# A retention block with a feed-forward behind it: a copy in another place, one k transposed by TensorE, natural k issued later

## The chip, the core and the metric

One core of a Trainium2 chip runs the whole program. The metric is the time of one execution on the device in microseconds (us); of several executions the median is given. Engines go by the names of the profile: PE is TensorE, DVE VectorE, ACT ScalarE, POOL GpSimd, SP SyncE (which here only issues transfers). ACT and POOL issue transfers too, and an engine's instructions run in the order of the program.

## What is computed

```python
# q, k, v: (8, 8, 576, 64) float32
scores = q @ k^T / 8
gamma  = 1 - 2 ** (-5 - arange(8))                    # one decay per head
D[s, t] = gamma ** (s - t) if s >= t else 0
x = ((scores * D) @ v), heads put side by side         # (4608, 512)
a, b = x @ w1, x @ w2                                  # (4608, 1024) each
out = ((a * b) @ w3) @ w_out                           # (4608, 512)
```

The weights and the inputs w1, w2, w3, w_out arrive as 64-bit floats and are turned into 32-bit ones on the chip; all products are in 32-bit.

## The kernel before

**Attention.** Batches are taken in pairs, and the 576 positions of a pair in five pieces (64, then 4 x 128). One piece of a pair is a *unit* `g`; there are 20, numbered from 0 (unit 10 is the eleventh, and the first, short piece of the third pair). Each unit needs k and q transposed (`kT`, `qT`), k as it lies in memory ("natural k", `ld_k`) for the running state, and v (`ld_v`). `state` (L240) adds k^T v to the state, `score` (L224) makes the masked scores `pm`, `pv` (L278) makes the unit's piece of x and copies it to `xT`. Transposed q and k come in two ways. Either SP loads the tensor in 32x32 blocks (`load_blocks`, L160: 8 or 16 transfers of 32 KB into a tile `bl_q` or `bl_k`; both kinds share two buffers with the tag `ld_q`) and DVE transposes the blocks (`front_blocks`, L185), or TensorE transposes natural k against an identity into PSUM and ACT copies it out (`front`, L207). `scale_blocks` (L175) lets POOL scale q.

**Feed-forward.** x is multiplied with w1 and w2 by Strassen's seven products: the first four of its twelve blocks of 384 tokens in `up` (L507), with one level; the other eight, in four groups of two, in `up2` (L1008), with two levels. w3 and w_out are multiplied once into `w3o`, and `down` (L625) multiplies a pair of token tiles with it, in seven products of four 128x256 matrix products each. Its first result is copied by ACT (L667), its sums are added by DVE (L641, L681), S4 is formed by DVE (L679), ACT copies one product out (L682) and issues the stores of the result tile `ot` (L710), of which there is one buffer.

**`up2`.** A group of tokens takes 14 multiplications of seven products; the seventh product is put off (`behind`) and issued by `finish()` inside the next `up2` or `down`. The sums of weights ("forms", 896 KB for a multiplication) are made once, sent to memory (`kept`, L882 to L888) and read back into a ring of three places (`next_forms`, L935: `ra<-kept`, L939). SP issues the first two of these loads in `open_second`, POOL all others, each in an `up2` for the multiplication after the next. The place ring[0] lies in the tile `ra` where the weights wA0 lay; ring[1], ring[2] and the two places `first` lie in the second tile `ra`, where the weights wA1 lay. The sums of tokens are made by POOL in `token_forms` (L942, operations at L948): `E` first, the forms `u` next; the last of the first group, `E4` (L969), comes in `rest()`, after a `down`. POOL also adds the second-level sums (L1033, `more`), DVE the others (L1038, L1040), and DVE multiplies a with b (L1003).

**Order.** Nothing is scheduled automatically. `work(n)` (L1099) takes the next `up`, `up2` or `down` from the list `todo`. Small steps are laid into lists which a multiplication empties as it goes: `aside`, `spread`, and `beside` (scaling of v by ACT). The stage change comes around unit 10: `down` on tiles (1,0),(1,1); loads for unit 10; `open_first` (L909), which sends the last weight forms; `token_forms(0)`; `down` on (2,2),(3,2); `open_second` (L921), which gives wA1's place to the ring and to `first`; `rest()`; and `down` on (3,0),(3,1), the first in which `second` is true. In it, and in every later `down`, L667 writes into `live["first"]` and not into `ot`; the stores and the product that the last `up2` left over come right behind it. Then `state(10)`, `score(10)` and the first `up2`, which begins with two 128x384 products that fill both `seed` buffers (L1016). Each later unit gets a number of multiplications (`dealt`, L1193); at its end come `pv(g)`, the loads of v and natural k for unit g + 2 by POOL (L1224, L1226), and state and score of unit g + 1. Units 11 to 13 (`whole`) get their transposed k from `front`.

Of the kernel before, what the change touches and what calls it, by code (L numbers as in the profile page):

```python
# [19 lines left out]
def kernel(  # L20
# [13 lines left out]
    nc = tc.nc  # L34
# [527 lines left out]

    aside, owed, spread, beside = [], [], [], []
    g = 0

    def w3_sums():
# [56 lines left out]
    def down(x, y, then=None, last=False):  # L625
        a, done, left = pair_of(x, y)
        second = "first" in live
        ahead(x, y)
        while len(done) < (1 if second else 3):
            aside.pop(0)()  # L630
        ps = {}
        ot = pools["ot"].tile([P, 2, 2, DM // 2], F32, tag="ot", name="ot")

        def product(nm, A, B, on=None):
            ps[nm] = ps[on] if on else acc.tile([P, DM // 2], F32, tag="acc", name="po")
            for f in range(NP):
                nc.tensor.matmul(ps[nm], a[A][:, f, :], live["W"][B][:, f, :], start=(f == 0 and not on),  # L637
                                 stop=(f == NP - 1), skip_group_check=True)

        def plus(nm, to, sb):  # L640
            nc.vector.tensor_add(ot[:, to[0], to[1]], ps[nm], ot[:, sb[0], sb[1]])  # L641
            if spread:
                spread.pop(0)()
            if second and aside and nm != 3:
                aside.pop(0)()

        def put(m, t, row, half=slice(0, 2)):

            i, n = every[m]
            r0 = t * P  # L650
            while r0 < (t + 1) * P:
                b = r0 // TB
                e = min((b + 1) * TB, (t + 1) * P)
                r = (2 * i + b) * S + n * TB + r0 - b * TB
                stores.append((out[r:r + e - r0, half.start * DM // 2:half.stop * DM // 2],
                               ot[r0 - t * P:e - t * P, row, half].rearrange("p h d -> p (h d)")))
                r0 = e
            if not keep_stores and not second:
                store()

        C11, C12, C21, C22 = (0, 0), (0, 1), (1, 0), (1, 1)
        product(1, "A11", "B11")
        first = ot[:, 0, 0]
        if second:
            first = live["first"].pop(0)
            live["first"].append(first)
        nc.scalar.copy(first, ps[1])  # L667
        if second:
            store()
            finish()  # L670
        product(7, "S3", "T3")
        if second:
            multiply()
        while len(done) < 3:
            aside.pop(0)()
        if then:
            ahead(*then)
        product(2, "A12", "B21", on=1)
        nc.vector.tensor_tensor(out=a["S4"], in0=a["A12"], in1=a["S2"], op=ALU.subtract)  # L679
        product(6, "S2", "T2")  # L680
        nc.vector.tensor_add(ot[:, 0, 1], ps[6], first)  # L681
        nc.scalar.copy(ot[:, 0, 0], ps[2])  # L682
        early = second or last or g >= 2 * NC - 1
        if early:
            put(*x, 0, slice(0, 1))
            store()
        plus(7, C21, C12)
        product(5, "S1", "T1")
        plus(5, C22, C21)
        product(4, "A22", "-T4")  # L690
        plus(4, C21, C21)
        put(*y, 1)
        if second:
            store()
        product(3, "S4", "B22", on=5)
        while aside and not early:
            aside.pop(0)()
        plus(3, C12, C12)
        put(*x, 0, slice(1 if early else 0, 2))
        if last:  # L700
            store()
        while aside:
            aside.pop(0)()
# [3 lines left out]
    def store():  # L707
        while stores:

            nc.scalar.dma_start(*stores.pop(0))  # L710
# [191 lines left out]
    ring, sent, steps, free = [], [0], [0], []  # L902
# [105 lines left out]
    def up2(gr, n):  # L1008

        h, key = n // 7, order[n % 7]  # L1010
        slot = ring[steps[0] % 3]
        if not steps[0]:

            for _ in range(2):
                t = pools["seed"].tile([P, 2, TB], F32, tag="seed", name="seed")
                nc.tensor.matmul(t.rearrange("p a t -> p (a t)"), ident, live["w3o"][:, 0, :2 * TB],  # L1016
                                 start=True, stop=True)
        B = live["B2", gr][OPERANDS[key][1]]
        steps[0] += 1
        c = free.pop(0)  # L1020
        sums2[key] = c
        add = {"P2": "P1", "P6": "P1", "P7": "P6", "P4": "P7", "P3": "P6"}.get(key)
        add = sums2[add] if add else None
        both = [sums2["P6"], sums2["P7"]] if key == "P5" else []

        def product(ps, a, b, new=False):
            for w in range(2):
                nc.tensor.matmul(ps[:, w, :], weight_of(slot, a, w), B[b], start=(new and w == 0), stop=True,  # L1028
                                 skip_group_check=True)

        def more(into, of, part):
            o, i = into[:, part], of[:, part]
            nc.gpsimd.tensor_tensor(out=o, in0=o, in1=i, op=ALU.add)  # L1033

        def plus(ps, j, with_add=None):
            if both:
                for o in both:
                    nc.vector.tensor_add(o[:, j], ps, o[:, j])  # L1038
            elif with_add is not None:
                nc.vector.tensor_add(c[:, j], ps, with_add[:, j])  # L1040
            else:
                nc.scalar.copy(c[:, j], ps)

        p1 = acc.tile([P, 2, TB], F32, tag="acc", name="up")
        product(p1, "A11", "B11", True)
        p6 = pools["seed"].tile([P, 2, TB], F32, tag="seed", name="seed")
        nc.scalar.copy(p6, p1)  # L1047
        store()
        p5 = acc.tile([P, 2, TB], F32, tag="acc", name="up")
        product(p5, "S1", "T1", True)  # L1050
        nc.scalar.copy(c[:, 3], p5)  # L1051
        finish()
        next_forms()
        product(p6, "S2", "T2")
        nc.scalar.copy(c[:, 1], p6)
        if beside:
            beside.pop(0)()
        for o in both:
            more(o, c, 3)
        if add is not None:  # L1060
            more(c, add, 3)
        product(p1, "A12", "B21")
        plus(p1, 0, add)
        product(p5, "S4", "B22")
        if add is not None:
            more(c, add, 1)
        for o in both:
            more(o, c, 1)
        product(p6, "S3", "T3")
        plus(p6, 3, c)  # L1070
        plus(p5, 1, c)
        if both:
            free.append(c)
        multiply(1 if both else 2)
        if n == 13:
            results.append((gr, h, 0, 1, c, 1))
        if aside:
            aside.pop(0)()

        def rest():  # L1080
            product(p6, "A22", "-T4")
            plus(p6, 2, add)
            if key in ("P6", "P3"):
                free.append(sums2["P1" if key == "P6" else "P6"])
            done = {"P2": (0, 0), "P4": (1, 0), "P5": (1, 1), "P3": (0, 1)}.get(key)
            if done:
                z = sums2["P7"] if key == "P5" else c
                results.extend((gr, h, *done, z, half) for half in ((0,) if n == 13 else (1, 0)))

        behind.append(rest)  # L1090
# [26 lines left out]
    g = NC  # L1117
# [48 lines left out]

    g = 2 * NC - 1
    work(1)
    for nm in "qk":
        load_blocks(g + 1, nm)  # L1170
    pv(g)()
    load(g + 2, "v", nc.scalar)
    load(g + 2, "k")
# [5 lines left out]
    g = 2 * NC  # L1179
    work(1)  # L1180
    rest()
    aside.extend(lambda nm=nm: front_blocks(g, nm) for nm in "qk")
    work(1)
    while aside:
        aside.pop(0)()
    ready = {2 * NC + 3: 1, 3 * NC + 1: 2, G - 1: 3}

    whole = range(2 * NC + 1, 2 * NC + 4)
# [5 lines left out]
    for g in range(2 * NC, G):  # L1194
        n = dealt[g - 2 * NC]
        if g + 1 < G:
# [6 lines left out]
            for nm in "qk":  # L1203
                blocks_in = nm == "q" or g + 1 not in whole
                if blocks_in:
                    aside.append(lambda nm=nm: front_blocks(g + 1, nm))
                work(1)
                while aside:
                    aside.pop(0)()
                if not blocks_in:  # L1210
                    front(g + 1, "k")
                if g + 2 < G and not (nm == "k" and g + 2 in whole):
                    load_blocks(g + 2, nm)
            work(tail)
            while beside:
                beside.pop(0)()
        else:
            work(n)
        pv(g)()
# [3 lines left out]
        if g + 2 < G:  # L1223
            load(g + 2, "v", nc.gpsimd)  # L1224
            if (g + 2) % NC != NC - 1:
                load(g + 2, "k", nc.gpsimd)  # L1226
        if g + 1 < G:
            state(g + 1)
            score(g + 1)
# [4 lines left out]
    g = G  # L1234
# [44 lines left out]
```

## Time and profile before

| | us |
|---|---|
| median of 5 runs | 861.39 |
| lowest and highest of them | 860.36, 876.87 |
| the profiled execution | 860.36 |
| its span, first to last instruction | 858.6 |
| granted TensorE clock, mean over the span | 0.991 |

| engine | busy us | share of the span |
|---|---|---|
| PE | 822.3 | 96% |
| DVE | 541.7 | 63% |
| POOL | 326.5 | 38% |
| ACT | 281.8 | 33% |

A profile line gives the start in us from the span's beginning, the length in us, the engine, the line of the program, the operation, the tile written and those read, the shape and the number of instructions, and in brackets the idle time of the engine before it with what ended that. An engine with a q behind its name (SPq, ACTq) stands for its issue of transfers. The waits view has who waited for whom, then us in total, how often, and the longest. Transfers have a time from issue to landing: the median is 5.0 us for the 54 loads `ra<-kept` that POOL issues.

### The profile page before, as it was taken

How to read it: one execution, taken by the hardware profiler on the slowest of the kernel's cores; microseconds unless marked ns; L12 is line 12 of the kernel's file. 1: busy time of each engine (PE TensorE's matmuls, PEld its weight loads, DVE VectorE, ACT ScalarE, POOL GpSimd, SP SyncE). 2: the span in 40 equal slices, each digit the busy share in tenths (PEclk: the TensorE clock that was granted, in tenths of full speed). 3: DMA queues.
4: the chain of work that ended last, by engine and by line, in shares of the span. 5: the costliest groups of instructions: out<-in, count | busy, mean ns of one | idle time of the engine just before them, and what ended most of it. 6: DMA issues, size and time to landing. Idle time of an engine off the chain costs nothing.

```text
span 858.6 us, 15769 instructions
## 1 busy us (share of the span) xinstructions
PE 822.3 (96%) x6077; PEld 739.3 (86%) x6077; DVE 541.7 (63%) x888; ACT 281.8 (33%) x579; POOL 326.5 (38%) x330
## 2 busy tenths in 40 slices
PE   9999999999999999499899999989999999999998
PEld 8899999644889998389898888988889998899987
DVE  4999999990744487335557643748744759446663
ACT  4777566771121111024244014242024331033300
POOL 1100010002004081567446754647925368535600
PEclk9999999999999999889999999999999999999999
DMA  9994454526055577979685437887355452245401
GB/s 190 224 225 115 76 152 119 148 74 110 13 111 104 101 250 232 280 191 219 169 232 162 68 81 201 224 214 196 66 110 196 152 206 68 83 147 178 166 25 50
DMA packets 203467, 127.22 MB, mean 148 GB/s; under 512 B 163448, under 2 KB 185208, under 8 KB 203392
## 3 DMA queue, kind: packets, MB, share of 16 engines
q1 hardware_dynamic: 173120, 50.40, 29.5%
q0 software_dynamic: 11776, 63.71, 22.9%
q10 hardware_dynamic: 18496, 12.10, 5.2%
q8 instruction: 48, 0.79, 0.4%
q14 instruction: 27, 0.22, 0.1%
HBM read 103.88 MB, written 22.28 MB: 147 GB/s over the span
## 4 chain that ended last, share of the span: by engine, by line
PE 75%; DMA 8%; DVE 8%; issue 4%; SPq 3%; ACT 1%; POOL 1%; DVEq 0%; ACTq 0%; POOLq 0%
PE po L637 22%; PE up L1028 15%; PE up L524 11%; PE seed L1028 11%; PE ps L477 6%; DMA ra<-kept 3%; PE xps L299 3%; DMA ld_v<-in_v_dram 3%; PE sc L233 3%; PE xps L274 1%; DVE c L529 1%; DVE ab L1003 1%; SPq L171 1%; SPq L882 1%; DMA kept<-wS 1%
## 5 line engine op out<-in xcount | busy, mean ns | idle before, releaser
L637 PE MATMUL po<-w3o,ab 128*128 128x256 f32 x552 | 127.0, 385 | 12.7 <-ACT ra L667 11.2
L637 PEld LDWEIGHTS po<-w3o,ab 128*128 128x128 f32 x552 | 105.0, 192 | 29.4 <-ACT ra L667 11.6
L1033 POOL TENSOR_TENSOR cc<-cc 128x384 f32<-128x384 f32 x112 | 109.5, 1004 | 4.0 <-ACT cc L1051 2.4
L1040 DVE TENSOR_TENSOR cc<-seed,cc 128x384 f32<-128x384 f32 x88 | 48.7, 553 | 73.6 <-PE seed L1028 71.5
L181 POOL TENSOR_TENSOR bl_q<-bl_q,gqs 128x512 f32<-128x512 f32 (+1 forms) x30 | 31.5, 1070 | 131.8 <-DMA bl_q<-in_q_dram 98.1
L939 POOL DMA_DIRECT2D ra<-kept x54 | 30.8, 570 | 128.4 <-PE seed L1028 102.5
L1028 PE MATMUL up<-xT,ra 128*128 128x192 f32 x384 | 73.5, 328 | 0.0
L524 PE MATMUL up<-xT,wA 128*128 128x192 f32 x384 | 70.7, 328 | 0.2 <-DVE xT L496 0.2
L1040 DVE TENSOR_TENSOR cc<-up,cc 128x384 f32<-128x384 f32 x88 | 48.4, 550 | 34.2 <-PE up L1028 28.6
L529 DVE TENSOR_TENSOR c<-up,c 128x384 f32<-128x384 f32 x80 | 44.0, 550 | 37.6 <-PE up L524 37.0
L637 PE MATMUL po<-wB,forms 128*128 128x256 f32 x288 | 65.4, 380 | 0.5 <-DVE forms L611 0.5
L236 DVE TENSOR_TENSOR pm<-sc,mask 128x512 f32<-128x512 f32 (+1 forms) x80 | 45.4, 626 | 31.8 <-PE sc L233 31.7
L524 PEld LDWEIGHTS up<-xT,wA 128*128 128x128 f32 x384 | 63.3, 190 | 1.6 <-issue 0.5
L1028 PEld LDWEIGHTS up<-xT,ra 128*128 128x128 f32 x384 | 63.8, 190 | 1.0
L637 PEld LDWEIGHTS po<-wB,forms 128*128 128x128 f32 x288 | 54.9, 191 | 8.4 <-PE po L637 0.8
L1028 PE MATMUL up<-ra 128*128 128x192 f32 x288 | 55.9, 331 | 6.3 <-DMA ra<-kept 6.2
L1047 ACT COPY seed<-up 128x384 f32<-128x384 f32 x56 | 26.0, 464 | 104.2 <-PE up L1028 48.7
L679 DVE TENSOR_TENSOR ab<-ab,forms 128x512 f32<-128x512 f32 x17 | 17.3, 1018 | 66.3 <-PE po L637 66.3
L477 PE MATMUL ps<-wo,w3T 128*128 128x512 f32 x128 | 55.1, 592 | 0.0
L1028 PE MATMUL seed<-e,ra 128*128 128x192 f32 x256 | 51.6, 330 | 3.5 <-DVE cc L1040 2.9
L1028 PEld LDWEIGHTS up<-ra 128*128 128x128 f32 x288 | 48.4, 192 | 7.5 <-DMA ra<-kept 6.0
L204 POOL TENSOR_TENSOR ld_v<-ld_v,gk 128x1024 f32<-128x1024 f32 (+1 forms) x9 | 17.4, 1930 | 91.6 <-DMA ld_v<-in_v_dram 91.6
(127 smaller groups left out, 1594.3 us busy)
## 6 DMA issues: line engine op xcount, KB each, us to landing
ra<-kept POOLq DMA_DIRECT2D x54, 896.0 KB, 5.0
raw<-in_moe_w_dram SPq DMA_DIRECT2D x72, 128.0 KB, 3.0
bl_q<-in_q_dram SPq DMA_DIRECT2D x216, 32.0 KB, 2.9
out_dram<-ot ACTq DMA_DIRECT2D x54, 128.0 KB, 2.3
bl_k<-in_k_dram SPq DMA_DIRECT2D x144, 32.0 KB, 3.0
raw<-in_moe_w_dram SPq DMA_DIRECT2D x16, 256.0 KB, 6.3
ld_k<-in_k_dram SPq DMA_DIRECT2D x8, 512.0 KB, 5.5
raw<-in_moe_w_out_dram SPq DMA_DIRECT2D x32, 128.0 KB, 2.7
```

What stands on the lines that cost most here:

```text
L181: nc.gpsimd.tensor_tensor(out=part, in0=part, in1=gqs[:, :, n0:n0 + n].unsqueeze(3).to_broadcast([P, NP, n, BL]), op=ALU.mult)
L233: nc.tensor.matmul(sc[j][:sz, p, :sz], kT[hs, b, p, :sz], qT[hs, b, p, :sz], start=True, stop=True)
L236: nc.vector.tensor_mul(pm[:sz, b, j, :, :sz], sc[j][:sz, :, :sz], mask[:sz, :sz].unsqueeze(1).to_broadcast([sz, NP, sz]))
L477: nc.tensor.matmul(ps, live["w3T", ft][:, g, :], live["wo"][:, g, :], start=(g == 0), stop=(g == KF - 1))
L524: nc.tensor.matmul(ps[:, w, :], a[:, w, r, :], b[:, r, :], start=(new and w == r == 0), stop=(w == r == 1), skip_group_check=True)
L529: nc.vector.tensor_add(c[:, to], ps, c[:, sb])
L637: nc.tensor.matmul(ps[nm], a[A][:, f, :], live["W"][B][:, f, :], start=(f == 0 and not on), stop=(f == NP - 1), skip_group_check=True)
L939: engine.dma_start(ring[n % 3], kept[n % 14 // 7][nm])
L1028: nc.tensor.matmul(ps[:, w, :], weight_of(slot, a, w), B[b], start=(new and w == 0), stop=True, skip_group_check=True)
L1033: nc.gpsimd.tensor_tensor(out=o, in0=o, in1=i, op=ALU.add)
L1040: nc.vector.tensor_add(c[:, j], ps, with_add[:, j])
L1047: nc.scalar.copy(p6, p1)
```

## The change

Three things are altered.

1. In the one `down` that comes before the first `up2` (`steps[0]` is 0), L667 writes into `ot[:, 0, 0]`, as it does in the downs of the first stage, and not into `live["first"]`. All later downs are as before.
2. Unit 10's k is not loaded in blocks. Its natural k, which was loaded for the state anyway, is transposed by TensorE: `front(10, "k")` stands behind that `down`. DVE's transpose of it goes, SP has 8 transfers fewer, and q of unit 11 takes the buffer that the blocks of k had.
3. The load of natural k for unit g + 2 is put into a list `loads`. The next `up2` issues it directly behind its own `next_forms()`, so on POOL it stands behind the load of weight forms and before the additions of L1033. If no `up2` comes in that unit, it is issued at the end of the unit's work, behind `scale_blocks` and `token_forms` (so for natural k of units 15 and 18). A unit whose k is transposed by `front` empties the list first.

```diff
-    aside, owed, spread, beside = [], [], [], []
+    aside, owed, spread, beside, loads = [], [], [], [], []
...
         first = ot[:, 0, 0]
-        if second:
+        if second and steps[0]:
             first = live["first"].pop(0)
...
         finish()
         next_forms()
+        if loads:
+            loads.pop(0)()
         product(p6, "S2", "T2")
...
     work(1)
-    for nm in "qk":
-        load_blocks(g + 1, nm)
+    load_blocks(g + 1, "q")
     pv(g)()
...
-    aside.extend(lambda nm=nm: front_blocks(g, nm) for nm in "qk")
+    aside.append(lambda: front_blocks(g, "q"))
     work(1)
     while aside:
         aside.pop(0)()
+    front(g, "k")
...
                 if not blocks_in:
+                    while loads:
+                        loads.pop(0)()
                     front(g + 1, "k")
...
-            while beside:
-                beside.pop(0)()
+            for left in (loads, beside):
+                while left:
+                    left.pop(0)()
...
-                load(g + 2, "k", nc.gpsimd)
+                loads.append(lambda g=g: load(g + 2, "k", nc.gpsimd))
```

## The prediction

> **What bounds the kernel now.** I read the page's busy times first, then who waited for whom, then the timeline where TensorE waits longest.
>
> ```profile
> PE 822.3 (96%) x6077; PEld 739.3 (86%) x6077; DVE 541.7 (63%) x888; ACT 281.8 (33%) x579; POOL 326.5 (38%) x330
> ```
>
> TensorE (PE) is busy for 96% of the span, so only its own work or its idle time can change the end. The waits view lists where it idles:
>
> ```profile
> PE po L637 <- ACT ra L667: 11.2, 1, 11.2
> ...
> PE up L1028 <- DMA ra<-kept: 6.2, 3, 2.8
> ```
>
> One wait of 11.2 us hangs on an ACT copy, three of 6.2 us together on the weight forms. The timeline of 318 to 400 us shows the first:
>
> ```profile
> 350.18 3.97 SPq L171 DMA_DIRECT2D bl_k<-in_k_dram  x8
> ...
> 350.50 3.72 PE L637 MATMUL po<-w3o,ab 128*128 128x256 f32 x16 [0.52 <-DVE ot L641]
> ...
> 363.50 1.77 SPq L939 DMA_DIRECT2D ra<-kept  x2
> 364.95 0.37 ACT L667 COPY ra<-po 128x256 f32<-128x256 f32 x1 [18.16 <-DMA kept<-wS]
> ...
> 365.38 3.78 PE L637 MATMUL po<-w3o,ab 128*128 128x256 f32 x8 [11.16 <-ACT ra L667]
> ...
> 366.95 1.80 POOL L948 TENSOR_TENSOR e<-xT,e 128x768 f32<-128x768 f32 x1
> ...
> 375.29 1.82 POOL L948 TENSOR_TENSOR e<-xT,e 128x768 f32<-128x768 f32 x1
> ...
> 377.05 0.62 POOL L939 DMA_DIRECT2D ra<-kept  x1
> ```
>
> TensorE ends two products at 354.22 and stands until 365.38. The copy writes into `ra`, which lies where the weights wA1 lay, and has to wait until the last of them has been sent to memory. The timeline of 392 to 416 us shows the largest of the three others:
>
> ```profile
> 395.26 1.20 POOL L93 DMA_DIRECT2D ld_v<-in_v_dram  x1 [2.00 <-PE xps L299]
> ...
> 396.46 1.17 POOL L93 DMA_DIRECT2D ld_k<-in_k_dram  x1
> ...
> 400.46 0.56 POOL L939 DMA_DIRECT2D ra<-kept  x1 [2.83 <-PE seed L1028]
> ...
> 410.25 1.65 PE L1028 MATMUL up<-ra 128*128 128x192 f32 x4 [2.79 <-DMA ra<-kept]
> 411.69 1.48 PE L1028 MATMUL up<-u,ra 128*128 128x192 f32 x4
> ```
>
> The form issued at 400.46 landed 9.7 us later, against a median of 5.0; v and k were ahead of it in GpSimd's queue. Behind the gap groups of four take 1.5 to 1.65 us instead of 0.81. Busy time by stretches prices gap and slow clock together, for two attention units with the same four multiplications (columns: length, PE, PEld, DVE, ACT, POOL, clock, DMA share, GB/s):
>
> ```profile
> 397.90:422.10 24.20, 21.41 (x124) 20.65 (x122) 12.84 (x23) 9.06 (x22) 13.76 (x16) 0.93 0.89 201
> 427.90:447.50 19.60, 19.57 (x122) 19.00 (x120) 11.52 (x21) 9.97 (x24) 10.44 (x13) 1.00 0.81 218
> ```
>
> That is 4.6 us, of which 2.79 are the gap and 1.8 the clock.
>
> **Part 1: the copy in its own place.** It now waits for product 1 (352.4) and for the stores of the pair of tiles before, which read the single `ot` buffer. Their last was issued at 350.5 and took 2.7 us: 353.2. With 0.37 us of copy it is done at 353.6, before TensorE asks at 354.22. The cover is only 0.6 us; each us of later stores would cost one. Five products of 8 matmuls at 0.216 us, 8.65 us, then follow at full clock (they took 10.75 behind the gap), and the pair ends at 362.9 instead of 376.1.
>
> **Part 2: k of unit 10 by TensorE.** Added are 8 transposes (the same 8 at 128 columns took 1.04 us; here 64, I take 0.9) and two ACT copies of about 0.33 us (as the 128x256 copies of L306), under the state products. One DVE transpose (0.70 us) goes, beside other work. SyncE loses 8 issues (3.97 us), so ld_k, the sends and the first two ring loads go out 4 us earlier: about 359.5 and 361, landed, at the 5.0 and 7.0 us of before, at 364.5 and 368. The load of q for unit 11 no longer waits for the buffer (372.65 before) and starts near 361; it may slow the second ring load by 1 us, which is not needed before 372. State, score and seeds took 3.4 us (376.1 to 379.5), so the first `up2` could start at 367.2, 12.3 us early.
>
> **What is late next** is GpSimd. Its chain of token forms starts when bl_q has landed (352.46), which neither part moves. E[0], for the second product, is ready at 368.75: up to 1 us of wait. E4, for the last product of the first `up2`, is ready at 377.1, and the load into the third ring place is queued behind it (377.05). The first `up2` then ends its six products near 372.4, the second does two (1.3 us) and stands from 373.7 to 377.2. Five products follow (3.25 us, plus 1.8 us of slow clock if the gap is treated as the one above): 382.2. The third `up2` needs the third ring place: 377.05 plus 5.0 (the median) to 6.7 us (this load before, with q loads beside it). I take 5.7, as the q of unit 11 is then in: 382.8. It started at 387.99 before. **Gain 5.2 us, from 3.6 to 6.0**, not the 12 that the gap suggests.
>
> Two rules of the Trainium skill bear on this. SBUF — State Buffer (Who interferes with whom) says that a DVE operation with two SBUF inputs holds up a GpSimd one that reads SBUF. The rows show that GpSimd can be slowed: the 128x384 sums take 0.98 us here, 1.44 in the later chains, under more DVE work. If any DVE work counted, the 3.6 us that now come under the chain (four masks, 1.41, and four additions of 0.55) would delay E4 by 1.6 us: the second chain took 25.2 us with 12.95 of DVE, this one 21.6 with 4.82, 0.44 us for each. By the rule, only L679 counts, which lay under the chain before as well (it took 1.47 instead of 0.69); the products' additions read PSUM. I take the rule, 0, and keep 1.6 for the range. TensorE: Matmul & The Clock Gate (Part 1) puts the fall to half clock at an idle window of about 3.4 us, running freely; by that the 2.79 us gap might have been free, but the row charges 1.8. I take the row for the new 3.5 us gap; by either sum the third ring place comes last, so it hides the loss.
>
> **Part 3: natural k behind the next form.** In four units (11, 12, 15, 16) the form now goes ahead of 512 KB; k's other two loads go behind a block of GpSimd work under the output products and are used later (that of unit 15 lands near 511 on the old clock, wanted at 515). GpSimd's form waits for TensorE anyway at 400.46 and 558.89, so there it isn't issued earlier, only freed of k's transfer; at 517.91 it followed k directly and comes 1.2 us earlier. Queued behind k's 1.17 us of issue are the additions of L1033, two q scalings and the next form: in unit 11 that one goes out near 406.2 instead of 405.0 on the old clock.
>
> - Unit 11: the form must land within 7.0 us; without k, and with the q loads earlier, I expect 5 to 6. The 4.6 us go. DMA: Bandwidth & Descriptors (Queues, rings and completion order) speaks against this: a ring is consumed in its order, so k, now behind this form, delays the next one. In the trace that form (405.01) took 9.2 us. By rule and bytes alone (v, k and two forms all in 16.3 us into the unit, at 414.2; the last wanted after three multiplications of 4.55 us and the transposes of k, 14.5) 1.8 us come back; by the share of q loads then gone, none. I take 4.5 (2.2 to 4.6).
> - Unit 12: 6.8 us before, no gap over 0.2: 0.
> - Unit 15: the form landed after 9.9 us, TensorE waited 1.17. Issued 1.2 us earlier, with only v ahead, it should take the 8.1 us of the form at 640.37, which had v alone ahead: gain 1.2 (0.6 to 1.3).
> - Unit 16: the form (9.1 us, gap 2.28) had v, k and 16 loads of bl_k beside it. The next took 8.5 us and landed 15.6 us into the unit; without the gap it is wanted at 13.65. So most comes back: 0.5 (0 to 2.4).
>
> **Sum.** 5.2 + 4.5 + 1.2 + 0.5 = 11.4 us. The profiled execution took 860.36 us (span 858.6 and 1.76 around it), so 849.0; the median of the five runs is 861.39, 1.0 above it, so I forecast 850.0 as a median.
>
> **The rivals.**
> - *The waits only move* (chance 0.20): k delays the second form in units 11, 15 and 16, and GpSimd's chain comes 1.6 us late. Gain 3.6 + 2.2 + 0.6 + 0 = 6.4: 855.0. For it: 9.2 and 8.5 us for those forms. Against: q loads are earlier by then.
> - *Most of the gap is kept* (0.04): the chain or third ring place doesn't bind; the third `up2` starts near 377, gain 11 + 6.2: 844. Against: GpSimd's order has E4 ahead of that load.
> - *Slower* (0.05): k in the ring makes the second form 2.8 us late in all four units, and the clock falls each time: (2.8 + 1.8) x 4 = 18.4, against 5.2 and the 8.1 us of old gaps removed: 866.5. It decides from 3.3 us per unit on. Against: unit 12 has no gap, though the same four transfers share its queue.
> - *No effect* (0.03): the stores or the ring hold TensorE until 365; 861. Against: they land at 353.2 and near 364.5, with other work between.
>
> **How the numbers follow.** The main case has 0.68; its terms span 6.4 to 14.3 us, and the range takes some of the first rival: 846.0 to 856.0. A difference under 0.2% (1.7 us) can't be told from none here. Faster 0.92, same 0.03, slower 0.05.
>
> **What would show it.** Right: no wait on L667; the new longest wait near there is TensorE on GpSimd (E4) for some 3.5 us, then under 1 us on the ring; the third `up2` 5 us earlier; unit 11 at 19.6 to 20 us. Wrong: L667 waiting on the stores, E4 after 379, or the second form of units 11 and 16 with waits over 2 us.

## The result, and the profile after

The changed kernel took 854.59 us (median of 23 executions, 849.51 to 859.90); the kernel before, beside it, 870.72 (44 executions, 858.85 to 877.30). The ratio is 0.9912, with an interval of 0.9887 to 0.9937. Executions of the kernel before lie at 858.9 to 865.0 and at 870.0 to 877.3, and the ratios here compare with the lower ones, but for a few executions up to 871.5. So the change is worth some 7.6 us of 861; 11.4 had been forecast.

The executions of the changed kernel fall into two groups: twelve from 849.5 to 854.6, eleven from 856.9 to 859.9. The profiled execution (857.14 us, span 855.4) is of the upper one. Its page, and its waits of TensorE over the whole span:

```profile
PE 822.0 (96%) x6085; PEld 738.8 (86%) x6085; DVE 546.7 (64%) x887; ACT 282.7 (33%) x581; POOL 326.1 (38%) x330
```

```profile
PE seed L1028 <- DVE cc L1040: 8.4, 4, 5.6
PE po L637 <- DVE ot L641: 3.4, 2, 2.9
...
PE po L637 <- ACT ot L667: 1.4, 2, 1.1
...
PE up L1028 <- DMA ra<-kept: 0.4, 1, 0.4
```

The wait of 11.2 us on L667 has shrunk to 1.1, and the three waits for weight forms (6.2 us) to one of 0.4. In their place stand one of 2.9 us on a sum of VectorE and one of 5.6 us on a sum for which GpSimd was late; the forecast had neither. Busy time by stretches shows unit 11, with the columns of the prediction:

```profile
403.46:423.25 19.79, 19.65 (x125) 18.98 (x122) 12.91 (x23) 9.06 (x22) 14.87 (x17) 1.00 0.86 220
```

Unit 11 now takes 19.79 us where it took 24.20, at full clock: gap and slow clock are both gone. So part 3 did what was expected, and the loss lies ahead of it. The timeline of 350 to 372 us:

```profile
351.02 3.72 PE L637 MATMUL po<-w3o,ab 128*128 128x256 f32 x16 [0.52 <-DVE ot L641]
355.42 0.37 ACT L667 COPY ot<-po 128x256 f32<-128x256 f32 x1 [8.71 <-DMA out_dram<-ot]
355.85 1.99 PE L637 MATMUL po<-w3o,ab 128*128 128x256 f32 x8 [1.11 <-ACT ot L667]
355.90 1.95 POOL L948 TENSOR_TENSOR xT<-xT 128x384 f32<-128x384 f32 x2
357.81 1.94 POOL L948 TENSOR_TENSOR ra<-xT 128x384 f32<-128x384 f32 x2
357.88 6.24 DVE L679 TENSOR_TENSOR ab<-ab,forms 128x512 f32<-128x512 f32 x1 [4.87 <-PE po L637]
359.72 3.85 POOL L948 TENSOR_TENSOR ra<-xT,ra 128x384 f32<-128x384 f32 x4
363.65 2.14 POOL L948 TENSOR_TENSOR xT<-xT 128x768 f32<-128x768 f32 x1
364.49 0.42 DVE L641 TENSOR_TENSOR ot<-po,ot 128x256 f32<-128x256 f32 x1
365.89 2.83 PE L637 MATMUL po<-w3o,ab 128*128 128x256 f32 x8 [2.87 <-DVE ot L641]
```

L667 waits for the stores until 355.42, not 353.2. S4 (L679), which takes 0.69 us undisturbed, is recorded for 6.24 us, beside six GpSimd additions at full speed (1.94 + 3.85 us for six, 0.96 each). It ends at 364.12, 0.47 us after the larger addition behind them (128x768) has started. TensorE stands 2.87 us, and its eight matmuls then take 2.83 us, where eight took 1.99 at 355.85: the granted clock is 0.60 over 365 to 375 us. The timeline of 376 to 396 us shows what that delay brings about:

```profile
377.82 0.34 ACTq L710 DMA_DIRECT2D out_dram<-ot  x1
...
383.01 11.53 SPq L171 DMA_DIRECT2D bl_q<-in_q_dram  x22
...
388.28 2.06 POOL L181 TENSOR_TENSOR bl_q<-bl_q,gqs 128x512 f32<-128x512 f32 x2 [10.17 <-DMA bl_q<-in_q_dram]
390.29 0.61 POOL L939 DMA_DIRECT2D ra<-kept  x1
390.92 1.95 POOL L1033 TENSOR_TENSOR cc<-cc 128x384 f32<-128x384 f32 x2
391.96 0.56 DVE L1040 TENSOR_TENSOR cc<-seed,cc 128x384 f32<-128x384 f32 x1 [6.90 <-POOL cc L1033]
...
392.57 1.65 PE L1028 MATMUL seed<-e,ra 128*128 128x192 f32 x4 [5.57 <-DVE cc L1040]
```

The last store of the pair is left in ACT's list and issued in the first `up2`, at 377.82. SyncE stands in the middle of the loads of q for unit 11 and goes on at 383.01; its waits have the reason:

```profile
SPq L171 <- DMA out_dram<-ot: 14.0, 3, 7.3
```

Of the q loads the eleventh waits 7.3 us, until that store has landed; in the trace it waits for the very semaphore that this store raises when it lands. q comes at 388.28 where the forecast counted on it before 382.8, and behind q's scaling GpSimd's form load and additions are queued, and behind those VectorE and TensorE.

A second profile of the changed kernel (no edit) fell into the lower group.

> The changed kernel once more, for a second profile. Its executions lie in two groups, 849.5 to 854.6 and 856.9 to 859.9. Theory A: if this one is of the lower group, S4 took at most 1.7 us, no wait of 5 us stands ahead of pv(10), and pv(10) starts near 391; if of the upper group, S4 took 5 us or more again. Theory B: the two groups differ elsewhere, with S4 alike in both.

It took 849.60 us (span 847.9). Its timeline:

```profile
355.07 0.37 ACT L667 COPY ot<-po 128x256 f32<-128x256 f32 x1 [7.11 <-DMA out_dram<-ot]
...
357.52 1.92 DVE L679 TENSOR_TENSOR ab<-ab,forms 128x512 f32<-128x512 f32 x1 [3.86 <-PE po L637]
357.90 2.39 POOL L948 TENSOR_TENSOR xT<-xT 128x384 f32<-128x384 f32 x2
...
369.31 0.34 ACTq L710 DMA_DIRECT2D out_dram<-ot  x1
```

and its waits of TensorE from 346 to 400 us:

```profile
PE up L1028 <- POOL e L948: 2.5, 1, 2.5
PE up L1028 <- DMA ra<-kept: 1.7, 1, 1.7
PE seed L1028 <- POOL e L948: 1.6, 1, 1.6
PE po L637 <- DVE ot L641: 0.5, 1, 0.5
```

S4 took a little more than the 1.7 us expected. It comes 0.4 us ahead of GpSimd's additions instead of 2.0 us behind their start. Two things moved: counted from the pair's start, S4 is 1.0 us earlier, and the chain, which comes behind the scaling of q of unit 10, is 1.35 us later. The last store goes out 8.5 us earlier, and what is late next is what the prediction named: E[0], E4, then the third ring place.

From the start of the pair to `pv(10)` it is 43.30 us in the kernel before, 48.34 in the upper profile, 38.84 in the lower one. This stretch is used below, since it doesn't depend on what lies ahead of it. Its busy times, upper and lower profile:

```profile
351.02:399.36 48.34, 38.40 (x220) 33.21 (x220) 17.71 (x24) 9.66 (x25) 32.00 (x31) 0.82 0.74 204
351.67:390.51 38.84, 32.98 (x220) 29.04 (x220) 13.52 (x24) 9.75 (x25) 31.97 (x31) 0.96 0.89 245
```

Of the 9.5 us between them, TensorE idles for 4.1 more (9.94 against 5.86), and 5.4 more go into the same 220 matmuls at a lower granted clock (0.82 against 0.96). So more than half of the difference is the clock, which is lower in the profile with the longer gaps.

### The profile page after: what moved, and what is told of

It reads as the page before. It is cut to its first block, busy times and chain, and to the rows that moved or that the text cites. A ratio compares the mean times of both kernels' runs of the same rounds, so it can differ in the third digit from the quotient of the medians.

```text
span 855.4 us, 15774 instructions
## 1 busy us (share of the span) xinstructions
PE 822.0 (96%) x6085; PEld 738.8 (86%) x6085; DVE 546.7 (64%) x887; ACT 282.7 (33%) x581; POOL 326.1 (38%) x330
## 4 chain that ended last, share of the span: by engine, by line
PE 76%; DMA 8%; DVE 7%; issue 4%; SPq 3%; ACT 2%; POOL 1%; ACTq 0%; DVEq 0%; POOLq 0%
PE po L637 22%; PE up L1028 14%; PE up L524 12%; PE seed L1028 11%; PE ps L477 6%; PE sc L233 3%; PE xps L299 3%; DMA out_dram<-ot 3%; SPq L171 2%; DMA ld_v<-in_v_dram 2%; PE xps L274 1%; DMA bl_q<-in_q_dram 1%; DVE ab L1003 1%; DVE c L529 1%; PE st L255 1%
## 5 line engine op out<-in xcount | busy, mean ns | idle before, releaser
L1033 POOL TENSOR_TENSOR cc<-cc 128x384 f32<-128x384 f32 x112 | 109.5, 1004 | 3.8 <-ACT cc L1051 2.4
L679 DVE TENSOR_TENSOR ab<-ab,forms 128x512 f32<-128x512 f32 x17 | 22.0, 1294 | 53.2 <-PE po L637 53.2
L1028 PEld LDWEIGHTS seed<-e,ra 128*128 128x128 f32 x256 | 43.0, 192 | 11.1 <-DVE cc L1040 9.5
```

## The experiments

**The theory**: L667's copy, late by the stores, decides whether S4 comes ahead of or behind GpSimd's chain (the two profiles show that the chain's own start has as much of a say); behind it, S4 is kept out, the stores go out later, and q of unit 11 waits for the last of them. **The rivals**: part 1, 2 or 3 fails by itself; the late q alone is the cause; S4's length is a mere lateness.

### One part alone

Part 1 alone, on the kernel before:

```diff
-        if second:
+        if second and steps[0]:
             first = live["first"].pop(0)
```

> The copy L667 in its own place alone; k of unit 10 by blocks and natural k as before. Theory A (the gain of the first two parts is eaten at unit 10 by S4, L679, which DVE cannot start while GpSimd's chain of token forms runs, and by a q load of unit 11 that SP holds back until a store of the output has landed): no wait of 11 us, L679 takes 5 us or more, TensorE waits some 3 us for L641; the first up2 starts near 376 to 378, and the second one waits for q again. Gain 0 to 4 us against before. Theory B (the loss comes from the sends that part 2 puts 4 us earlier, which make the stores land late): without part 2 the stores land in 2.7 us, L679 takes 0.7 to 1.5 us, first up2 near 369, gain 6 to 9 us.

Measured: 870.01 us, ratio 1.0022 (0.9966 to 1.0078). Four of its twelve executions lie at 859.3 to 862.3, eight at 869.6 to 875.4, and the ratio has some of both. Its profile (of 875.41 us, which matters below) has no wait on L667 in the pair, and the timeline of TensorE shows what came instead:

```profile
371.56 1.62 PE L1028 MATMUL up<-xT,ra 128*128 128x192 f32 x4 [4.90 <-DMA ra<-kept]
383.55 0.92 PE L1028 MATMUL up<-ra 128*128 128x192 f32 x4 [0.63 <-DMA ra<-kept]
389.56 1.65 PE L1028 MATMUL seed<-e,ra 128*128 128x192 f32 x4 [4.45 <-DVE cc L1040]
```

The first form isn't there, since SyncE has the k blocks ahead of it, and q of unit 11 is late. Pair to `pv(10)`: 45.27 us, 2.0 more than before. Neither theory had this: S4 took 1.36 us, where A expected 5 or more, and the first `up2` came at 371.56, where B expected 369.

Part 2 alone:

```diff
-    for nm in "qk":
-        load_blocks(g + 1, nm)
+    load_blocks(g + 1, "q")
...
-    aside.extend(lambda nm=nm: front_blocks(g, nm) for nm in "qk")
+    aside.append(lambda: front_blocks(g, "q"))
...
+    front(g, "k")
```

> k of unit 10 transposed by TensorE alone; L667 still writes into ra. The copy waits until the last send has landed, 3.5 to 4 us earlier than before (361 in place of 365). Theory A: S4 comes near 365 instead of 369, in the thick of GpSimd's chain, takes 3 us or more, and q of unit 11 waits for the stores: gain 0 to 2 us, or a loss of up to 2. Theory B: gain 2.5 to 3.5 us (4 less 0.9 for the transposes).

Measured: 860.36 us, ratio 0.9901 (0.9836 to 0.9966). The wait on L667 fell from 11.2 to 8.0 us, because the last weights are sent earlier; pair to `pv(10)` 41.74, a gain of 1.56. That is in theory A's range, but not by its reason, as S4 took 1.66 us at 366.62. The rest of the ratio is not seen in its profile (span 859.0 against 858.6).

Part 3 alone, with the three places that empty the list as in the change:

```diff
-                load(g + 2, "k", nc.gpsimd)
+                loads.append(lambda g=g: load(g + 2, "k", nc.gpsimd))
```

> Natural k behind the next form alone. Theory A: as in the changed kernel, units 11, 12, 15 and 16 give back 4.4, 0.3, 1.7 and 1.9 us: 8 us less than before, no wait of TensorE on a form over 0.5 us. Rival (the gain in unit 11 came because q loads stood elsewhere in time in the changed kernel, or the second form comes late instead): gain under 5 us, with a wait on a form in unit 11 or 16 over 1 us.

Measured: 855.22 us, ratio 0.9875 (0.9820 to 0.9929). The wait on L667 is there as before (11.7 us) and units 11, 15 and 16 lose their waits for forms but for 0.6 us in two. So part 3 is worth all that the whole change gained in its median.

Parts 1 and 3 without part 2 (the first and the third of these diffs together):

> Parts 1 and 3 without part 2: unit 10's k still comes in blocks. Theory A (part 2's use is that SyncE issues the two ring loads 4 us earlier and the q load of unit 11 sooner; part 3 works by itself): the copy at L667 runs near 354 as in the run with part 1 alone, the first up2 again waits about 5 us on ra<-kept near 371.5, pv(10) starts near 394, about where it did before, and units 11, 15 and 16 give the 8 us that part 3 gave alone: median 853 to 856, no shorter than part 3 alone by more than 1.5 us. Theory B (the three parts add up and part 2 is not needed for part 1): median near 851, with pv(10) near 391.

Measured: 858.48 us, ratio 0.9984 (0.9964 to 1.0005). The wait of 4.86 us for the first form is back, with 2.23 and 2.92 us behind it; pair to `pv(10)` 43.91. Theory A holds for the place, so part 1 works only with part 2; its size doesn't, as the kernel is 2.5 us above the range. In its profile some 3 us are lost at 703 to 724, where VectorE's products L1003 (one took 3.68 us instead of 0.5) meet GpSimd's chain of the last group.

### The last store at the pair's end

```diff
-        if last:
+        if last or second and not steps[0]:
             store()
```

> The changed kernel, with the last store of the first pair (the half row that the first up2 issues) issued at the end of that pair instead. Theory A (the load of q for unit 11 stands on SP until that store has landed at 383, because the two share a semaphore): the q load is issued through by 381, GpSimd's scaling starts by 382, TensorE's wait of 5.6 us in the second up2 is gone with the slow clock behind it: 6 to 7 us less than the changed kernel as profiled (857), so 850 to 851. Rival (the q load is late because the DMA engines are full with ring loads and sends): the scaling still starts at 387 to 388, no difference over 1 us to the changed kernel.

Measured: 851.24 us (848.50 to 853.04), ratio 0.9826 (0.9773 to 0.9880), faster than both kernels. In its profile q's scaling starts at 378.54 instead of 388.28. S4 took 1.65 us there, so the profile alone does not tell what the store would have been worth with S4 late; the six executions, none in the upper group, do. Nor is there one above 854.5 among the 22 of the four kernels below and here that have the last store at the end.

### GpSimd's chain behind S4

```diff
         nc.vector.tensor_tensor(out=a["S4"], in0=a["A12"], in1=a["S2"], op=ALU.subtract)
+        if second and not steps[0]:
+            nc.gpsimd.tensor_copy(live["E"][:, 0, 0, 0, :1], a["S4"][:, 0, :1])
+            token_forms(0)()
...
-    rest = token_forms(0)
...
-    rest()
```

> The changed kernel, with GpSimd's first chain of token forms (L948) held back until S4 (L679) is formed: one element of S4 is copied by GpSimd ahead of it. The last store stays where it was, so L667 still waits for stores and the q load of unit 11 still waits for the last one. Theory A (in the profiled execution of the changed kernel, S4 came 1 us late and then lost the SBUF port to GpSimd's additions for 6.2 us; from there come 5 of the lost us): S4 takes at most 1.7 us, no wait of TensorE on L641 over 1 us in that pair, the chain starts 1.5 to 2.5 us later, so E[0] and E4 cost TensorE 1 to 2 us more than in the best run; median 851 to 854, no execution above 856. Theory B (the shared wait of the q load on the last store, or the late stores themselves, cost the 5 us): wait of 5 us before pv(10) stays, median near 857.

Measured: 850.44 us (849.25 to 855.51), ratio 0.9895 (0.9865 to 0.9926). L667 still made TensorE wait 1.07 us, the last store still goes out in the first `up2`, but at 368.30, and S4 is short, in the timeline of 354 to 362 us:

```profile
356.55 0.69 DVE L679 TENSOR_TENSOR ab<-ab,forms 128x512 f32<-128x512 f32 x1 [4.83 <-PE po L637]
...
357.40 0.18 POOL L681 COPY e<-ab 128x1 f32<-128x1 f32 x1 [1.88 <-DVE ab L679]
357.54 1.95 POOL L951 TENSOR_TENSOR xT<-xT 128x384 f32<-128x384 f32 x2
```

With S4 out of the way the late L667 costs nothing in the end: 40.30 us to `pv(10)`, and no wait of 5 us. Theory A, with a median a little below its range. Both edits together:

> The changed kernel with both edits: the last store of the first pair at that pair's end, and GpSimd's first chain of token forms held back until S4 is formed. Theory A (two separate causes, S4 behind GpSimd's additions and the q load of unit 11 behind the last store, make the upper half of the changed kernel's executions): each edit alone already takes that half away, so both together are at 849 to 851.5 with no execution above 854; E[0] and E4 still cost TensorE 2.3 to 2.8 and 1.5 to 1.6 us. Theory B (the spread of the changed kernel has another cause): executions at 856 to 860 come back.

Measured: 852.40 us (850.12 to 854.43), ratio 0.9873 (0.9844 to 0.9902). No execution of the upper group; the median is 0.9 us above theory A's range and one execution is above 854. By ratio it lies between the two edits alone: together they add nothing, so each is enough.

### S4 made late

Two copies of S2 by VectorE ahead of S4, on the kernel with the last store at the end:

```diff
+        if second and not steps[0]:
+            for _ in range(2):
+                nc.vector.tensor_copy(ot[:, 1].rearrange("p h d -> p (h d)"), a["S2"].rearrange("p f t -> p (f t)"))
         nc.vector.tensor_tensor(out=a["S4"], in0=a["A12"], in1=a["S2"], op=ALU.subtract)
```

> The changed kernel with the last store of the first pair at that pair's end, and two copies on VectorE (S2 into the not yet used half of ot, 128x512, together about 1 us) ahead of S4 in that pair. Theory A (whoever starts first keeps the port; GpSimd's additions follow one another without a gap): S4 starts behind GpSimd's first L948 (356.2), takes 4 to 7 us instead of 1.65, TensorE waits 2 to 3.5 us on L641, the first up2 starts 6 to 9 us later than at 367, and the time is 3 to 7 us above that of the same kernel without the copies: 854 to 858. Theory B (VectorE and GpSimd share the port fairly; S4 is merely 1 us late): 0 to 1.5 us more, 851 to 852.5.

Measured: 851.10 us (847.76 to 854.23), ratio 0.9888 (0.9859 to 0.9917). The edit missed its aim: in the profile GpSimd's chain itself started only at 357.69, behind S4 (357.06, 1.26 us). It says nothing on the theory.

With the chain's start set by data, S4 behind seven copies from PSUM, and the last store at the end:

```diff
+        if second and not steps[0]:
+            nc.vector.tensor_copy(ot[:, 1, 0], ps[2])
+            nc.gpsimd.tensor_copy(live["E"][:, 0, 0, 0, :1], ot[:, 1, 0, :1])
+            token_forms(0)()
+            for _ in range(7):
+                nc.vector.tensor_copy(ot[:, 1, 1], ps[2])
```

> The changed kernel with the last store at the pair's end, and the meeting of S4 and GpSimd's chain set by data: the chain waits for a copy that VectorE makes right behind product 2 (some 356.5), and S4 comes behind seven more such copies from PSUM (0.42 us each), so some 3 us into the chain, in the middle of its six 128x384 additions into ra. Theory A (in these additions, which follow one another without a gap, an instruction of VectorE with two SBUF inputs is not let in): S4 takes 3.5 to 6 us and ends with the sixth addition near 365; TensorE waits 3 to 4.5 us on VectorE before the last products of the pair; time 3 to 6 us above that of the kernel with both edits. Theory B (VectorE is let in at the next instruction's end): S4 takes at most 1.7 us, is done before TensorE needs it (some 361), and costs nothing; time within 1.5 us of that kernel.

Measured: 853.85 us (849.35 to 854.08), ratio 0.9876 (0.9841 to 0.9911). S4 started 2.8 us into the chain and took 0.68 us. This contradicts theory A as it was put: lying in those additions isn't enough. Forty trials by themselves, behind the last output:

```diff
+    for trial in range(40):
+        k = trial % 20
+        nc.vector.tensor_copy(s[:, 0, :1], E[:, 0, 0, 0, :1])
+        nc.gpsimd.tensor_copy(E[:, 1, 1, 1, :1], s[:, 0, :1])
+        for j in range(8):
+            nc.gpsimd.tensor_tensor(out=outs[j if trial >= 20 else 7], in0=E[:, 0, 1], in1=E[:, 1, 0], op=ALU.add)
+        for _ in range(4 + k // 7):
+            nc.vector.memset(U[3], 0.0)
+        nc.vector.memset(U[3].rearrange("p a t -> p (a t)")[:, :16 + 48 * (k % 7)], 0.0)
+        nc.vector.tensor_tensor(out=U[0], in0=U[1], in1=U[2], op=ALU.add)
```

> The changed kernel with the last store at the pair's end, and forty trials behind its last output, so the time is some 350 us longer and only the trials are read. In each trial GpSimd makes eight additions of 128x384 (some 0.96 us each) and VectorE, behind fills that take no input, one addition of 128x384 with both inputs in SBUF (some 0.55 us alone). Its start is shifted by some 50 ns from trial to trial, over about one addition of GpSimd. In the first twenty GpSimd writes one place over and over (each instruction waits on the one before), in the last twenty eight places (six follow without any wait). Theory A (an instruction of VectorE that comes while GpSimd's additions follow one another is kept out to their end, whenever it comes): the additions take 3 to 6 us in all twenty of the second kind, and at most 1.5 us in the first. Theory B (it is let in at the next end of an instruction): at most 1.5 us in all forty. Theory C (which of the two happens hangs on where in GpSimd's instruction it comes): in both kinds, or in the second, some trials at most 1.5 us and some over 3 us, neighbours in time alike.

The row of that addition (shortest, median and longest in ns):

```profile
L1255 DVE TENSOR_TENSOR u<-u x40: 494/680/1372, 850.0 to 1192.5; 128x384 f32<-128x384 f32 x40
```

The shortest took 494 ns, the longest 1372: never more than one addition of GpSimd was waited for, with or without waits between these. Theory B, in the trials. So nothing of S4's 6.24 us came back in them, where VectorE went from its own work into the addition. What was not yet tried was S4 as it is in the kernel, coming from a wait for product 2, only later. Three kernels copy product 1 three, six and nine times more on ScalarE ahead of L667:

```diff
+        if second and not steps[0]:
+            for _ in range(3):
+                nc.scalar.copy(ot[:, 1, 1], ps[1])
         nc.scalar.copy(first, ps[1])
```

> The changed kernel with three more copies of product 1 on ScalarE ahead of the copy at L667 in the first pair (into a half of ot that is overwritten later), some 1.1 us. Product 2 waits for that copy, so S4 comes some 1.1 us later; GpSimd's chain starts where it did. Theory A (S4 is kept out by GpSimd's additions when it comes 1 to 3 us after their start): S4 comes some 0.8 us after the start, into the second addition; it takes at most 1.9 us in some executions and 5 to 6 in others, time 851 to 860. Theory B (S4's lateness costs only itself): S4 at most 1.9 us, time 850.5 to 853.

> The same with six copies, some 2.2 us. Theory A: S4 comes some 2 us after the chain's start, as in the slower profile of the changed kernel, takes 5 to 6 us, TensorE waits 2.5 to 3.5 us on VectorE before its last products, the store of the pair's last half goes out after 375, q of unit 11 comes late; time 858 to 862. Theory B: S4 at most 1.9 us, time 851.5 to 854.5.

> The same with nine copies, some 3.3 us. Theory A: S4 comes some 3 us after the chain's start and takes 4 to 5 us, up to the end of the sixth addition into ra; time 858 to 863. Theory B: S4 at most 1.9 us, time 852.5 to 856.

| copies | us, median (executions) | ratio | S4 behind the chain's start | S4 took | q's scaling | pair to `pv(10)` |
|---|---|---|---|---|---|---|
| 3 | 855.44 (9) | 0.9931 (0.9891 to 0.9970) | 3.3 | 4.90 | 386.29 | 45.44 |
| 6 | 854.62 (5) | 0.9925 (0.9889 to 0.9960) | 3.7 | 4.49 | 387.76 | 42.13 |
| 9 | 852.93 (5) | 0.9906 (0.9873 to 0.9939) | 4.5 | 3.69 | 380.97 | 38.47 |

The timeline of the kernel with six copies, VectorE and GpSimd:

```profile
361.12 1.94 POOL L951 TENSOR_TENSOR ra<-xT 128x384 f32<-128x384 f32 x2
362.93 4.49 DVE L682 TENSOR_TENSOR ab<-ab,forms 128x512 f32<-128x512 f32 x1 [6.69 <-PE po L637]
363.02 3.85 POOL L951 TENSOR_TENSOR ra<-xT,ra 128x384 f32<-128x384 f32 x4
366.94 2.14 POOL L951 TENSOR_TENSOR xT<-xT 128x768 f32<-128x768 f32 x1
```

In all three profiles S4 ends 0.47 to 0.48 us after the first 128x768 addition has started, whenever it began: 365.80 to 365.33, 367.42 to 366.94, 366.52 to 366.05; in the changed kernel's own upper profile 364.12 to 363.65. So S4 was kept out to the end of the chain's 128x384 additions, four times of four. That much of theory A holds. Its times do not: the kernel with nine copies has S4 late and long, and `pv(10)` at 38.47 us as in the best profile. There the last store went out at 375.29 and q still came at 380.97: no q load waits for that store in the trace, as it landed in 1.8 us and the one load that shares its semaphore was issued only later. With three and six copies q came 5 to 7 us later, and TensorE waited 2.57 and 1.67 us for it. With six it wasn't the last store either: SyncE stood 7.0 us, until 373.75, for the pair's first one. Within these runs the lost time goes with q's arrival more than with S4's length. By medians theory A is wrong for six and nine copies (858 to 863 expected) and fits three; theory B is wrong in S4's length in all.

### Natural k of unit 18 alone

The kernel before, with part 3's list for unit 18 only, emptied where `beside` is:

```diff
-                load(g + 2, "k", nc.gpsimd)
+                loads.append(lambda g=g: load(g + 2, "k", nc.gpsimd))
+                while loads and g + 2 != 18:
+                    loads.pop(0)()
```

> The kernel before, with one edit: natural k of unit 18 alone is issued as part 3 does it, behind the q scaling and the third chain of token forms. Theory A (the executions of the kernel before that take some 11 us more are those in which three multiplications a*b at L1003 lose the SBUF port to that chain, 14.3 us instead of 3.2; GpSimd's chain now starts 1.2 us earlier and misses them): all executions between 857 and 865, median 861, longest L1003 under 3 us. Theory B (those executions have another cause): executions above 868 stay as frequent as in the kernel before beside it, median near that of it; at most 1 us less from unit 17.

Measured: 862.05 us (12 executions, 856.70 to 867.16), ratio 1.0011 (0.9985 to 1.0036). It gains nothing. That no execution is above 868 (9 of 23 of the kernel before beside it are) fits theory A, though two are above its 865. The longest L1003 is 2.7 us in its profile and in that of the kernel before alike, but neither is of an execution above 868. The profile of part 1 alone is, with 875.41 us:

```profile
599.15 14.29 DVE L1003 TENSOR_TENSOR ab<-cc 128x384 f32<-128x384 f32 x3
599.22 2.08 POOL L181 TENSOR_TENSOR bl_q<-bl_q,gqs 128x512 f32<-128x512 f32 x2
601.24 1.95 POOL L948 TENSOR_TENSOR xT<-xT 128x384 f32<-128x384 f32 x2
603.14 1.93 POOL L948 TENSOR_TENSOR ra<-xT 128x384 f32<-128x384 f32 x2
605.04 3.83 POOL L948 TENSOR_TENSOR ra<-xT,ra 128x384 f32<-128x384 f32 x4
608.95 2.00 POOL L948 TENSOR_TENSOR xT<-xT 128x768 f32<-128x768 f32 x1
...
614.09 2.50 PE L637 MATMUL po<-w3o,ab 128*128 128x256 f32 x5 [11.37 <-DVE pm L236]
```

The first of these three products took 10.14 us (0.53 alone), beside two scalings and eight additions of GpSimd without a gap, and TensorE stood 11.37 us. From `pv(16)` to `pv(17)` it is 58.37 us there and 44.72 in the kernel before, 13.7 of the 15.0 us between the two spans. So theory A's cause is seen in one such execution. The counts go with it: of the kernel before 23 of 44 executions lie at 870 or more, of part 1 alone eight of twelve above 868 and of part 2 alone five; of the 89 of the changed kernel and those that keep part 3 (the trials apart) none is above 862.

## Why the prediction was right or wrong, point by point

The change is faster, as expected, but the forecast of 850.0 us is 4.6 below the median. The lower group is near the forecast, in part by luck, as the terms below are off in both directions: the second profile took 849.60 us where the sum had given 849.0. Sums against the kernel before, by stretches of the profiles (us gained):

| term | predicted | lower profile | upper profile |
|---|---|---|---|
| pair to `pv(10)` (parts 1 and 2) | 5.2 | 4.46 | -5.04 |
| unit 11 | 4.5 | 4.07 | 4.41 |
| unit 12 | 0 | 0.30 | 0.29 |
| unit 15 | 1.2 | 1.53 | 1.69 |
| unit 16 | 0.5 | 1.43 | 1.90 |
| what lies ahead of the pair | 0 | -1.17 | -0.52 |
| all other stretches | 0 | 0.08 | 0.47 |
| span | 11.4 | 10.7 | 3.2 |

- **Part 3, right.** 7.3 to 8.3 us instead of 6.2. The second form behind k in the queue never held TensorE in unit 11. The consumption of a ring in order, which the Trainium skill states for the queues of SyncE and ScalarE (DMA: Bandwidth & Descriptors, Queues, rings and completion order), was no price on GpSimd's queue, where the next form had time: at 411.69 it was issued 5.1 us behind k, and no wait on a form is seen in unit 11. The "waits only move" rival falls, and unit 16 was mis-sized by 0.9 to 1.4 us on the careful side. What the forecast did not have: with natural k of unit 18 behind the chain, the executions of 870 us and more are gone, so over all executions the median fell by 16 us and not by 7.6.
- **Part 1, the step that failed**: "Their last was issued at 350.5 and took 2.7 us: 353.2", and with it "The cover is only 0.6 us; each us of later stores would cost one." The 2.7 us were those of the kernel before. The store took 4.3 us in the upper and 3.0 in the lower profile, so the copy came 4.4 and 3.4 us after the pair's start instead of 3.1, and the cover was overrun or just used up. In the five profiles without part 2 this store took 2.5 to 2.9 us, in the twelve with it 2.8 to 4.3: part 2 brings the load of natural k (350.41 instead of 354.24) and the sends behind it to beside this store. The sum put that at nothing; that it is the reason is likely, but no run tests it alone. And a microsecond here is worth nothing or ten. TensorE lost 1.1 us directly in the upper profile; the rest of the 9.5 us between the two profiles of one kernel comes by S4, the stores, q and the clock behind the gaps. That L667 might wait was among the things named as proving the forecast wrong; what it would lead to was not worked out.
- **"By the rule, only L679 counts, which lay under the chain before as well", wrong twice.** In the kernel before S4 came after the pair's 11 us of waiting, at 369.20, when GpSimd was at its larger sums, and took 1.47 us; the change brought it to 355 to 358, to the start of the chain. And the rule was taken only as a delay of GpSimd. SBUF — State Buffer (SBUF: two separate sides) says that whichever of the two starts first gets the shared pair for its whole instruction and the other is blocked. If the one that waits comes next, S4 waits for at most one addition, 0.96 us. The forty trials (at most 1.37 us, with its own 0.49) agree. In nine profiles S4 came ahead of the chain, in its first 0.6 us, or behind VectorE's own copies, and took at most 2.05 us; the longest lost the rest of a scaling and one addition. The four rows in which it came from a wait for TensorE 2.0 to 4.5 us into the chain, 3.69 to 6.24 us, do not agree: it was blocked through four to six instructions. Nor does the row of L1003 with 10.14 us, blocked through ten. The measurement decides.
- **"The q of unit 11 is then in", right only if the last store is early.** The store was nowhere in the sum, as it was counted with the pair. It is issued in the first `up2`, and SyncE's loads can wait for it; with the store at 369.31 no wait for q is seen, with the store at 377.82 one of 5.6 us. Nine copies show the limit of this: what counts is whether a q load needs a store's semaphore before that store has landed.
- **What is late next, right in order, off in size.** E[0], 2.5 us (up to 1 was expected), E4, 1.6 (3.5), the third ring place, 1.65. The start of the chain, "which neither part moves", did move: it came 6.2 us after the pair's start in the lower profile, 5.0 before. In sum it came out close: the third `up2` starts at 384.89, which is 383.7 on the clock of the pair before (382.8).
- **Part 2, right and needed.** Without it part 1 gives nothing (45.27 us to `pv(10)`, and 43.91 with part 3, against 43.30 before). It also is what seems to make the store of part 1 late.

**What stays open.** Why a waiting VectorE instruction is kept out through many GpSimd additions in some places and let in at the next in others. Coming from a wait isn't the difference: S4 behind VectorE's own copies was let in at once, 2.8 us into the chain, but L1003 in the profile of part 1 alone came behind VectorE's own work too and was kept out for ten instructions. That S4 and q are both needed for the whole 9.5 us is what the edits that take away one of them show; the split into idle time and clock is read from two profiles.

## What to carry to other kernels

When a stall is removed, ask which instructions behind it now meet another engine's chain, and look at both sides of a shared port: the short instruction beside a back-to-back chain may be the one that waits. A cover of half a microsecond is not a small risk times one; follow what is queued behind the instruction that becomes late, down to the transfer that waits for it. A store that is put off into a later stage is part of the change's critical path if a load waits on it.

## What had not been expected of the hardware

- One VectorE subtraction with two SBUF inputs (0.69 us alone) took 3.69 to 6.24 us beside GpSimd additions that ran at full speed (0.96 us each), in four profiles, always to the end of the chain's 128x384 additions. A product of VectorE (0.53 us alone) took 10.14 us in the same way in a fifth.
- The same kind of instruction took at most 1.37 us in forty trials beside eight such additions.
- An issue of SyncE waited up to 7.3 us for a store that ScalarE had issued, with neither data nor buffer in common: q's loads write `bl_q`, the store reads `ot`. In this program the two share a semaphore that tells of landing.
